# A long convolution by FFT: merged spectrum products, two copies on another engine, no idle matmuls

## The chip, the cores and the metric

The kernel runs on one core of a Trainium2 chip. Its engines run side by side, each through its own queue in order: TensorE (PE, with its weight loads shown apart as PEld) multiplies matrices into PSUM; VectorE (DVE), ScalarE (ACT) and GpSimd (POOL) work elementwise; SyncE (SP) and POOL issue the DMAs here. The metric is the device time in microseconds of one execution. Before the change it is 2101.66 us, the median of three runs (2099.22 to 2106.14).

## The reference

Two steps on `x` of 8 x 5696 x 128. First a causal convolution along the sequence, done with FFTs of twice its length; then a mixing layer with two 5696 x 5696 matrices.

```python
def _attn_ref(x, h):
    B, S, D = x.shape
    L = 2 * S
    Xf = np.fft.rfft(x, n=L, axis=1)
    Hf = np.fft.rfft(h, n=L, axis=0)
    Yf = Xf * Hf[None, :, :]
    return np.fft.irfft(Yf, n=L, axis=1)[:, :S, :].astype(np.float32)

def _moe_ref(x, w_theta, w_tok_r, w_tok_i, w_ch):
    theta = x @ w_theta
    zr, zi = x * np.cos(theta), x * np.sin(theta)
    yr = np.einsum('ts,bsd->btd', w_tok_r, zr)
    yi = np.einsum('ts,bsd->btd', w_tok_i, zi)
    u = x + yr + yi
    return (u + np.maximum(u @ w_ch, 0.0)).astype(np.float32)
```

## The kernel before

**The FFT as matmuls.** The transform of length 11392 is factored into 178 x 64. The filter `h` goes through the first two stages once; its spectrum is parked in HBM (`hf_hbm`). Then come eight groups, each two batch entries (`bp`) and half of the 128 channels (`dh`), with `dh` changing fastest. The text numbers them 0 to 7; the even ones have `dh` 0. A group has four stages:

- *Stage A* (L194): 64 matmuls of 180 columns, with slices of `x16` as weights, 4 to a PSUM tile; the 16 tiles are copied to `a_` on ScalarE (L201).
- *Stage B* (`stage_b`): 12 chunks over the 90 frequencies, 8 in each of the first 11 and 2 in the last. `f2` (L212) does a chunk's second transform in 32 matmuls (8 in the last); ScalarE copies the PSUM tile to `xs` (L310); VectorE multiplies `xs` twice by the filter's spectrum `hs`, once with its real part into `u_t` and once with its imaginary part into `v_t` (L312). `hs` comes by two DMAs a chunk on SP's queue, four chunks ahead (`LEAD`), into four buffers.
- *Stage C* (L328, L329): 256 matmuls that read all of `u_t` and `v_t` as weights, 16 to a PSUM tile; VectorE, and ScalarE for four tiles, evict them to `g` (L336, L333, L334). A matmul of stage C reads columns from every chunk, so that none can start before the last product of stage B.
- *Stage D* (`stage_d`, L351): the last inverse transform in 7 chunks over the 64 phases, 10 in each of the first 6 (20 matmuls) and 4 in the last; ScalarE copies each PSUM tile to `yt` (L354), 890 elements per partition in a full chunk, and `yt` goes to HBM.

**What runs beside what.** `woven` interleaves lists of steps by their place between 0 and 1, and a scheduler then sets the order on each engine. Stage C of a group is woven with stage A of the next, and stage B of the next group with stage D of this one. In the last group there is no next one: its stages C and D are woven with phase steps (the `theta`, sine and cosine part of the mixing layer). All these stages share one pool of four PSUM tiles, used in turn; `xs` has two buffers.

**The idle matmuls.** Behind the last chunk of stage B, and likewise behind the last chunk of the filter's pass, `f2` issues `WARM` = 12 matmuls of 384 columns (L218) whose results are not read. They write to free columns of the last chunk's PSUM tile and read `w_t2`.

**Setup.** Before the groups, tables of sines and cosines are made by POOL (L150, L152), VectorE (L155, L156, L163) and ScalarE (L160, L167): `w_t2`, `r_u`, `r_v`, `e_t`. The filter's chunks are scaled on VectorE or ScalarE in turns (L246, L248).

**The mixing layer** follows: phase steps, and from about 560 us on the products with the token matrices, in two passes of Strassen-like sums (L1099), whose weights POOL's queue loads into a ring of six buffers (L509) that takes the place of `w_t2`.

Of the kernel before, what the change touches and what calls it, by code (L numbers as in the profile page):

```python
# [12 lines left out]
F16 = mybir.dt.float16  # L13
add = mybir.AluOpType.add
mult = mybir.AluOpType.mult
AF = mybir.ActivationFunctionType
# [6 lines left out]
def kernel(  # L23
# [10 lines left out]
    nc = tc.nc  # L34
    B, S, D = x.shape
    assert D == 128
    P = 128
# [42 lines left out]
    K1 = N1 // 2 + 1  # L80
    CK = 8
    HD = D // 2
    EN = N2 // 2 + 1
    WARM = 12
    assert N1 * N2 == NF and NB * N2 == S and NB % 2 == 1 and K1 <= P
    CHK = [(c0, min(CK, K1 - c0)) for c0 in range(0, K1, CK)]
    NCK = len(CHK)
    CN = 10
    CHN = [(c0, min(CN, N2 - c0)) for c0 in range(0, N2, CN)]
    UVW = 2 * HD * K1  # L90
# [6 lines left out]
    def psum():  # L97
        return fp.tile([P, 2, 512], F32, tag="ps", name="ps")
# [3 lines left out]
    def pool(name, bufs, stack, **kw):  # L102
        return stack.enter_context(tc.tile_pool(name=name, bufs=bufs, **kw))
# [6 lines left out]
    fc = pool("fft_c", 1, conv, side="right")  # L110
# [1 line left out]
    s1 = pool("set_1", 1, setup, side="right")  # L112
    s2 = pool("set_2", 2, setup, side="right")

    u_t = fc.tile([P, UVW + P], F16)
    v_t = fc.tile([P, UVW + P], F16)
    uv = [t[:, :UVW].rearrange("p (e d k) -> p e d k", e=2, k=K1) for t in (u_t, v_t)]
    h16 = s1.tile([P, 2, N2, HD], F16)
    for p0, p1 in ((0, 80), (80, NB)):
        nc.gpsimd.dma_start(u_t[p0:p1, :N2 * D],  # L120
# [22 lines left out]
    def turns_of(pattern, base, lanes, m, per, quarter=None):  # L143

        n = 1
        for _, c in pattern:
            n *= c
        t = s2.tile([P, 11 * NB], F32, tag="turn", name="turn")[:m, :n]
        k = s2.tile([P, 11 * NB], F32, tag="whole", name="whole")[:m, :n]
        nc.gpsimd.iota(k, pattern=pattern, base=base, channel_multiplier=0,  # L150
                       allow_small_or_imprecise_dtypes=True)
        nc.gpsimd.tensor_scalar(t, k, lanes, 1.0 / per, op0=mult, op1=mult)  # L152
        if quarter is not None:
            quarter(t)
        nc.vector.tensor_scalar(k, t, MAGIC, None, op0=add)  # L155
        nc.vector.scalar_tensor_tensor(t, k, MAGIC, t, op0=ALU.subtract, op1=ALU.subtract)  # L156
        return t, k
# [12 lines left out]
    t, k = turns_of([[1, K1]], 0, lane[:NB, 1:2], NB, N1)  # L170
# [3 lines left out]
    w_t2 = keep.tile([P, K1, 3 * N2], F16, tag="keep", name="w_t2")  # L174
# [29 lines left out]
    def f2(a_st, c):  # L204

        c0, ck = CHK[c]
        ps = psum()
        for j in range(ck):
            for ri in range(2):
                for e in range(2):  # L210
                    rows = slice(64 * e, 64 * e + 64)
                    nc.tensor.matmul(ps[:, e, j * HD:(j + 1) * HD],  # L212
                                     w_t2[rows, c0 + j, N2 * (1 - ri):N2 * (3 - ri)],
                                     a_st["a"][rows, ri * K1 + c0 + j, :],
                                     start=(ri == 0), stop=(ri == 1))
        if c == NCK - 1:
            for n in range(WARM):
                nc.tensor.matmul(ps[:, n % 2, ck * HD:ck * HD + 384], w_t2[:, 2, :P],  # L218
                                 w_t2[:, 0:2, :].rearrange("p k n -> p (k n)"), start=True, stop=True)
        return ps[:, :, :ck * HD].rearrange("p e (k d) -> p e d k", k=ck)  # L220

    def woven(*lists):
# [17 lines left out]
    def h_chunk(c):  # L240
        c0, ck = CHK[c]
        ps = f2(a_h, c)
        h_ = hst[c // 6][:, c % 6]
        dst = h_[:, :, :, :ck]
        if c % 2:
            nc.vector.tensor_scalar(dst, ps, 16.0 / NF, None, op0=mult)  # L246
        else:
            nc.scalar.activation(dst, ps, AF.Copy, scale=16.0 / NF)  # L248
        for cc, j in ((0, 0), (NCK - 1, CHK[-1][1] - 1)):
            if c == cc:  # L250
                nc.vector.tensor_scalar(dst[:, :, :, j], dst[:, :, :, j], 0.5, None, op0=mult)
        for ri in range(2):
            nc.sync.dma_start(
                hf_hbm[:, c, :, ri, :].rearrange("h p n -> p h n"),
                h_[64 * ri:64 * ri + 64].rearrange("p h d k -> p h (d k)"))

    for c in range(NCK):
        h_chunk(c)
    nc.gpsimd.memset(u_t[:, UVW:], 0.0)
    nc.gpsimd.memset(v_t[:, UVW:], 0.0)  # L260

    r_u = fc.tile([P, P], F16)
    r_v = fc.tile([P, P], F16)
# [30 lines left out]
    def stage_b(a_st, dh):  # L294

        hs_of = {}

        def load(c):
            if c >= NCK:
                return  # L300
            hs = hs_of[c] = fh.tile([P, 2, HD * CK], F16, tag="hs", name="hs")
            for e in range(2):
                nc.sync.dma_start(hs[64 * e:64 * e + 64], hf_hbm[dh, c])

        def chunk(c):
            c0, ck = CHK[c]
            hv = hs_of[c].rearrange("p r (d k) -> p r d k", k=CK)
            ps = f2(a_st, c)
            xs = fs.tile([P, 2, HD, CK], F16, tag="xs", name="xs")
            nc.scalar.activation(xs[:, :, :, :ck], ps, AF.Copy)  # L310
            for r in range(2):
                nc.vector.tensor_tensor(  # L312
                    uv[r][:, :, :, c0:c0 + ck], xs[:, :, :, :ck],
                    hv[:, r:r + 1, :, :ck].to_broadcast([P, 2, HD, ck]), op=mult)
            load(c + LEAD)
        return [lambda c=c: load(c) for c in range(LEAD)], [lambda c=c: chunk(c) for c in range(NCK)]
# [22 lines left out]
    def stage_d(st, bp, dh, then=None):  # L339
        def chunk(n0, cn):  # L340
            if n0 == 0:
                st["yt"] = fg.tile([P, NB, N2], BF16, tag="yt", name="yt")
            g_, yt = st["g"], st["yt"]
            ps = psum()
            nq = 5 if cn == CN else cn
            for j in range(cn):
                n = n0 + j
                o = ps[:, j // nq, (j % nq) * NB:(j % nq + 1) * NB]
                for ri in range(2):
                    e_ = e_t[:K1, n, ri, :] if n < EN else e_t[:K1, N2 - n, ri, ::-1]  # L350
                    nc.tensor.matmul(o, g_[:K1, ri * N2 + n, :], e_, start=(ri == 0), stop=(ri == 1))  # L351
            y_out = yt[:, :, n0:n0 + cn].rearrange("p m (a q) -> p m a q", q=nq)
            y_in = ps[:, :cn // nq, :nq * NB].rearrange("p a (q m) -> p m a q", q=nq)
            nc.scalar.activation(y_out, y_in, AF.Copy)  # L354
            if n0 + cn == N2:
                if then is not None:
                    then(yt)
                if then is not None:
                    gate = nc.gpsimd.tensor_copy(small(0, 1)[HD:HD + 1], sides["phases"][1][HD:HD + 1, 3, H - 1:H]).ins
                for e in range(2):  # L360
                    t0 = H if then else 0
                    with tc.issue_after(gate) if then else ExitStack():
                        (nc.gpsimd if then else nc.sync).dma_start(
                            yt_hbm[dh * HD:(dh + 1) * HD, 2 * bp + e, t0:],
                            yt[64 * e:64 * e + 64].rearrange("p m n -> p (m n)")[:, t0:])
        return [lambda n0=n0, cn=cn: chunk(n0, cn) for n0, cn in CHN]
# [125 lines left out]
    def small(at, n):  # L492
        return ring["all"][:, WB + BT + at:WB + BT + at + n]
# [436 lines left out]
    for i, (k, p, tt, j0, s0, nj) in enumerate(stretches):  # L930
# [38 lines left out]
        if tt is None:  # L969
            if p:  # L970
                aside(True, False)
            if first_of_pair:
                q = M1 if p else M3
                ps = mps.tile([P, 512], F32, tag=f"m{q}", name=f"m{q}")
# [3 lines left out]
            for j in range(nj):  # L978
                jj = j0 + s0 + j
                for r in range(2):  # L980
# [3 lines left out]
                    for k_ in range(2):  # L984
                        for h, t in enumerate(terms):
                            nc.tensor.matmul(ps[64 * h:64 * h + 64], t[2 * k_][:, j, :64, r], b[t[2 * k_ + 1]],  # L986
                                             start=st_ and k_ == 0, stop=sp_ and k_ == 1)
# [6 lines left out]
            if end_of_pair:  # L994
# [5 lines left out]
                c, c0 = c_last  # L1000
# [48 lines left out]
        if classic:  # L1049
            for n in range(4):  # L1050
# [4 lines left out]
                if end_of_pair and n % 2:  # L1055
                    (c12, z12), (c21, z21), (c11, z11), (c22, z22) = cs
                    out_of = (((c11, z11, 0), (c12, z12, 1)), ((c21, z21, 2), (c22, z22, 3)))[n // 2]
                    for h, (c, z, m_) in enumerate(out_of):
# [6 lines left out]
                        else:  # L1065
                            for b in range(4):
                                nc.tensor.matmul(ms[m_][:, b * D:(b + 1) * D], z[:, b, :], ident_bf,
                                                 start=False, stop=(b == 3))
# [11 lines left out]
        else:  # L1080
# [13 lines left out]
            for n, q in enumerate(ORDER):  # L1094
                sum_some(1)
                for j in range(nj):
                    jj = j0 + s0 + j
                    for r in range(2):
                        nc.tensor.matmul(ms[q], a[q][:, j, :, r], bts[jj][q][:, r, :],  # L1099
                                         start=(jj == 0 and r == 0),  # L1100
                                         stop=(jj == NJ - 1 and r == 1 and q not in left))
# [60 lines left out]
```

## Time and profile before

| | |
|---|---|
| median of three runs | 2101.66 us |
| span of the profiled execution | 2098.1 us |
| PE busy | 1979.5 us, 94% |
| DVE busy | 1595.2 us, 76% |
| ACT busy | 675.3 us, 32% |
| POOL busy | 912.5 us, 43% |
| first stage C to last (L328, first starts) | 88.4 to 388.8 us |
| idle matmuls (L218) | 108, from 50.7 to 384.6 us |
| xs copies (L310) on ACT | 96, 96.6 us busy |
| spectrum products (L312) on DVE | 192; those of 1024 elements 736 and 756 ns in the mean |
| yt copies (L354) on ACT | 48 of 890 elements, 927 ns; 8 of 356, 530 ns |
| stage C evictions (L336) on DVE | 92, of 1.21 to 1.30 us in the mean |

A line of the page's groups reads: source line, engine, operation, what it writes and reads with partitions x elements and type, count; then busy time, mean duration in ns; then the engine's idle time just before these instructions and what ended it. The view of one line lists the shortest, median and longest duration and who waited for it. In the timeline each row has its start and length in us. In the rows by stretches the busy time of PE, PEld, DVE, ACT and POOL (with counts) is followed by the TensorE clock that was granted as a share of full speed, the DMA engines' busy share and GB/s.

### The profile page before, as it was taken

Reading aid. Unit: us, or ns where it says so; the run is one execution under the profiler, and the core shown is the slowest. Engines: PE = TensorE matmul, PEld = TensorE weight load, DVE = VectorE, ACT = ScalarE, POOL = GpSimd, SP = SyncE. Lnnn points to the kernel's source line nnn. Section 1 sums busy time; section 2 is a strip of 40 time slices with the busy share of each in tenths; the row PEclk is TensorE's granted clock in tenths of the full one; section 3 lists DMA queues with packets and bytes.
Section 4 is the critical chain, followed back from the end, with each engine's and each line's share of the span. In section 5 each row is a group of like instructions: output and inputs, shape, how many; then the busy total and the mean of one; then the engine's idle time right before and its main releaser. Section 6 shows DMA issues by size and latency. Waiting matters only on the chain.

```text
span 2098.1 us, 41505 instructions
## 1 busy us (share of the span) xinstructions
PE 1979.5 (94%) x15688; PEld 1109.4 (53%) x15865; DVE 1595.2 (76%) x2881; ACT 675.3 (32%) x995; POOL 912.5 (43%) x1662
## 2 busy tenths in 40 slices
PE   4888999878999999999999999899999999999998
PEld 3788888754444444444444444344444444444444
DVE  7777776776878888888886766886777777777867
ACT  5887877874332333333310000011111111111111
POOL 5301010327444636354557554435354545445450
PEclk8799999989999999999999999999999999999999
DMA  7357474989989989898999989869797887879693
GB/s 144 94 137 175 123 171 121 239 243 239 179 153 179 178 175 168 171 173 177 171 175 152 154 167 284 136 107 156 127 154 132 148 142 136 154 130 155 126 155 89
DMA packets 408233, 334.97 MB, mean 160 GB/s; under 512 B 85895, under 2 KB 358407, under 8 KB 407047
## 3 DMA queue, kind: packets, MB, share of 16 engines
q0 software_dynamic: 225952, 156.72, 52.8%
q1 hardware_dynamic: 176096, 164.05, 27.3%
q10 hardware_dynamic: 5984, 11.54, 1.6%
q8 instruction: 124, 2.03, 0.4%
q14 instruction: 77, 0.63, 0.1%
HBM read 377.11 MB, written 92.49 MB: 224 GB/s over the span
## 4 chain that ended last, share of the span: by engine, by line
PE 63%; DVE 4%; DMA 2%; issue 2%; POOL 0%; ACT 0%; DVEq 0%
PE m L1099 59%; DVE c L1106 2%; DMA ring<-in_moe_w_tok_r_dram 1%; DVE b L655 1%; PE v L801 1%; PE utp L794 1%; PE m L1103 1%; DVE wt L714 1%; PE tpz L742 0%; PE theta_ps L396 0%; POOL ring L509 0%; PE m L986 0%; DMA yT<-yt_hbm 0%; PE m L1020 0%; DMA zl<-zl_hbm 0%
## 5 line engine op out<-in xcount | busy, mean ns | idle before, releaser
L509 POOL DMA_DIRECT2D ring<-in_moe_w_tok_i_dram x720 | 390.8, 557 | 653.0 <-DVE wt L714 579.6
L509 POOL DMA_DIRECT2D ring<-in_moe_w_tok_r_dram x720 | 389.0, 559 | 145.8 <-DVE wt L714 85.5
L714 DVE STREAM_TRANSPOSE wt<-ring 128x384 f32<-128x384 f32 (+2 forms) x720 | 359.3, 523 | 110.3 <-PE m L1099 70.0
L1099 PE MATMUL m<-b,wt 128*128 128x512 bf16 x1599 | 385.9, 380 | 4.1 <-DVE wt L714 1.7
L1099 PEld LDWEIGHTS <-wt 128*128 128x128 bf16 x1804 | 176.4, 98 | 219.7 <-DVE wt L714 7.8
L1106 DVE TENSOR_TENSOR c<-c,m 128x512 f32<-128x512 f32 x412 | 265.2, 669 | 0.4 <-PE m L1099 0.4
L796 ACT ACTIVATE ring<-utp 128x512 bf16<-128x512 bf16 x85 | 50.8, 597 | 582.3 <-PE utp L794 582.3
L328 PE MATMUL ps<-r_u,u_t 128*128 128x128 f16 x1024 | 126.4, 223 | 6.4 <-ACT red L419 3.0
L329 PE MATMUL ps<-r_v,v_t 128*128 128x128 f16 x1024 | 125.5, 223 | 0.4
L1020 PE MATMUL m<-b,wt 128*128 128x512 bf16 x466 | 110.2, 381 | 8.9 <-DMA b<-z_hbm 4.9
L791 ACT ACTIVATE ub<-c 128x512 bf16<-128x512 f32 x88 | 55.0, 628 | 191.5 <-DMA ring<-in_moe_w_tok_r_dram 113.0
L130 POOL DMA_DIRECT2D x<-in_x_dram x64 | 33.9, 536 | 184.9 <-PE ps L194 174.8
L328 PEld LDWEIGHTS <-u_t 128*128 128x128 f16 x1024 | 103.4, 101 | 5.5 <-DVE u_t L312 4.6
L329 PEld LDWEIGHTS <-v_t 128*128 128x128 f16 x1024 | 102.4, 100 | 4.4 <-issue 2.4
L310 ACT ACTIVATE xs<-ps 128x1024 f16<-128x1024 f32 x96 | 96.6, 1030 | 14.7 <-DVE v_t L312 6.7
L312 DVE TENSOR_TENSOR u_t<-xs,hs 128x1024 f16<-128x1024 f16 x96 | 68.6, 715 | 29.2 <-ACT xs L310 19.0
L1020 PEld LDWEIGHTS <-wt 128*128 128x128 bf16 x528 | 51.1, 99 | 69.2 <-issue 9.6
L194 PE MATMUL ps<-f_t,x 89*128 89x180 f16 x512 | 77.2, 298 | 4.0 <-ACT xs L310 2.6
L212 PEld LDWEIGHTS <-w_t 64*128 64x128 f16 x3240 | 60.8, 102 | 37.5 <-issue 24.5
L398 ACT ACTIVATE red<-theta_ps,magic 128x512 f32<-128x512 f32 (+1 forms) x46 | 31.6, 687 | 134.6 <-PE theta_ps L396 104.5
L194 PEld LDWEIGHTS <-x 89*128 89x128 f16 x512 | 70.8, 241 | 5.5 <-issue 4.5
L744 ACT ACTIVATE ring<-tpz 128x512 bf16<-128x512 bf16 (+1 forms) x46 | 27.5, 597 | 131.9 <-PE tpz L742 113.0
(2895 smaller groups left out, 3868.9 us busy)
## 6 DMA issues: line engine op xcount, KB each, us to landing
ring<-in_moe_w_tok_r_dram POOLq DMA_DIRECT2D x352, 96.0 KB, 4.5
ring<-in_moe_w_tok_i_dram POOLq DMA_DIRECT2D x352, 96.0 KB, 4.9
ring<-in_moe_w_tok_r_dram POOLq DMA_DIRECT2D x352, 80.0 KB, 4.5
ring<-in_moe_w_tok_i_dram POOLq DMA_DIRECT2D x352, 80.0 KB, 3.9
hs<-hf_hbm SPq DMA_DIRECT2D x192, 128.0 KB, 3.1
cp_hbm<-c SPq DMA_DIRECT2D x88, 256.0 KB, 2.5
c<-cp_hbm SPq DMA_DIRECT2D x88, 256.0 KB, 4.4
out_dram<-c SPq DMA_DIRECT2D x88, 256.0 KB, 4.5
```

Source lines behind the costliest of these rows:

```text
L194: nc.tensor.matmul(ps[:, i // 2, (i % 2) * 2 * K1:(i % 2 + 1) * 2 * K1], lhs(q + i), f1_t[:NB], start=True, stop=True)
L212: nc.tensor.matmul(ps[:, e, j * HD:(j + 1) * HD], w_t2[rows, c0 + j, N2 * (1 - ri):N2 * (3 - ri)], a_st["a"][rows, ri * K1 + c0 + j, :], s ...
L310: nc.scalar.activation(xs[:, :, :, :ck], ps, AF.Copy)
L312: nc.vector.tensor_tensor(uv[r][:, :, :, c0:c0 + ck], xs[:, :, :, :ck], hv[:, r:r + 1, :, :ck].to_broadcast([P, 2, HD, ck]), op=mult)
L328: nc.tensor.matmul(o, u_t[:, at:at + P], r_u, start=True, stop=False)
L329: nc.tensor.matmul(o, v_t[:, at:at + P], r_v, start=False, stop=True)
L509: nc.gpsimd.dma_start(wb[32 * i:32 * i + 32, :ng, :nj * 64], bass.AP(tensor=a.tensor, offset=a.offset + row0 * S + p * H + i * QR + j0 * 6 ...
L714: nc.vector.transpose(wt.rearrange("p j t r -> p (j t r)").bitcast(F32).rearrange("p (j g t) -> p g j t", j=TJ, g=4)[:, :ng, :nj], wb[:, : ...
L791: nc.scalar.activation(ub[:m].rearrange("p b d -> p (b d)"), c[:m], AF.Copy)
L1020: nc.tensor.matmul(ms[n // 2 * 2 + h], a[n][:, j, :, r], bts_of[p][jj][n % 2 * 2 + h][:, r, :], start=(n % 2 == 0 and jj == 0 and r == 0), ...
L1099: nc.tensor.matmul(ms[q], a[q][:, j, :, r], bts[jj][q][:, r, :], start=(jj == 0 and r == 0), stop=(jj == NJ - 1 and r == 1 and q not in left))
L1106: nc.vector.tensor_tensor(c, z, ms[q], op=op)
```

## The change

It has three parts, all in the FFT. The idle matmuls are gone. `u_t` and `v_t` become two views of one tile `uv_t`, so that the first 11 chunks of each stage B form both products in one VectorE instruction of 2048 elements, which reads `xs` and `hs` with broadcast strides; the last, short chunk keeps two. Of stage D's seven copies those of the first and the fourth chunk go to VectorE.

```diff
-    WARM = 12
...
-    u_t = fc.tile([P, UVW + P], F16)
-    v_t = fc.tile([P, UVW + P], F16)
-    uv = [t[:, :UVW].rearrange("p (e d k) -> p e d k", e=2, k=K1) for t in (u_t, v_t)]
+    uv_t = fc.tile([P, 2 * UVW + P], F16)
+    u_t, v_t = uv_t[:, :UVW + P], uv_t[:, UVW:]
+    uv = uv_t[:, :2 * UVW].rearrange("p (r e d k) -> p (r e) d k", r=2, e=2, k=K1)
...
-        if c == NCK - 1:
-            for n in range(WARM):
-                nc.tensor.matmul(ps[:, n % 2, ck * HD:ck * HD + 384], w_t2[:, 2, :P],
-                                 w_t2[:, 0:2, :].rearrange("p k n -> p (k n)"), start=True, stop=True)
...
-    nc.gpsimd.memset(u_t[:, UVW:], 0.0)
-    nc.gpsimd.memset(v_t[:, UVW:], 0.0)
+    nc.gpsimd.memset(uv_t[:, 2 * UVW:], 0.0)
...
-            for r in range(2):
+            if ck == CK:
                 nc.vector.tensor_tensor(
-                    uv[r][:, :, :, c0:c0 + ck], xs[:, :, :, :ck],
+                    uv[:, :, :, c0:c0 + ck],
+                    xs.rearrange("p e d k -> p e (d k)").unsqueeze(1).to_broadcast([P, 2, 2, HD * CK]),
+                    hv.rearrange("p r d k -> p r (d k)").unsqueeze(2).to_broadcast([P, 2, 2, HD * CK]), op=mult)
+            for r in range(2 if ck < CK else 0):
+                nc.vector.tensor_tensor(
+                    uv[:, 2 * r:2 * r + 2, :, c0:c0 + ck], xs[:, :, :, :ck],
                     hv[:, r:r + 1, :, :ck].to_broadcast([P, 2, HD, ck]), op=mult)
...
-            nc.scalar.activation(y_out, y_in, AF.Copy)
+            if n0 in (0, 3 * CN):
+                nc.vector.tensor_copy(y_out, y_in)
+            else:
+                nc.scalar.activation(y_out, y_in, AF.Copy)
```

The last 38 columns that stage C's last matmul on `u_t` reads behind its end were zeros and are now `v_t`'s first columns; the rows that they make are not read.

## The prediction

> **What bounds the kernel now.** I read the profile in this order: the costliest groups, to see which of the edited lines are large; the lines' own views (who waits for them); the timeline across one group boundary; and sums over hand-cut stretches. The chain of waits comes last and says that, from 597 us on, the weight-mixing matmuls of L1099 set the end (59% of the span); the change does not touch them. The edited code ends at about 440 us, so all that it can do is to start the rest earlier or later, one for one. In that part the eight groups follow each other every 42 to 44 us (stage C's first matmul at 88.4, 131.1, 173.2, 216.3, 258.4, 303.0, 345.6 and 388.8 us). Each is a stage C of 21.4 to 22.9 us, followed by a stage of B and D woven, about 20.6 us from its first matmul to the next group's stage C.
>
> ```profile
> L310 ACT ACTIVATE xs<-ps 128x1024 f16<-128x1024 f32 x96 | 96.6, 1030 | 14.7 <-DVE v_t L312 6.7
> L312 DVE TENSOR_TENSOR u_t<-xs,hs 128x1024 f16<-128x1024 f16 x96 | 68.6, 715 | 29.2 <-ACT xs L310 19.0
> ```
>
> These page lines are the chain in stage B: ScalarE copies a chunk out of PSUM (xs), VectorE multiplies it twice. VectorE waits 19.0 us in all for that copy, ScalarE 6.7 us for VectorE: both are nearly full, neither is the bound alone. The view of the idle matmuls of L218:
>
> ```profile
> L218 PE MATMUL ps<-w_t x108: 326/326/527, 50.7 to 384.6; 128*128 128x384 f16 x108
> ...
>   ACT xs L310: 2.7, 3
>   DVE v_t L246: 1.6, 1
> ```
>
> They write into the last chunk's PSUM tile, so the copy of that chunk must wait for them: 2.7 us in three groups. The timeline at the end of the fourth group shows how (start, length, engine, line; in brackets the idle time before it):
>
> ```profile
> 211.97 2.12 PE L218 MATMUL ps<-w_t 128*128 128x384 f16 x12
> 212.01 1.02 ACT L310 ACTIVATE xs<-ps 128x1024 f16<-128x1024 f32 x1 [0.20 <-PE ps L212]
> ...
> 213.68 1.17 DVE L312 TENSOR_TENSOR v_t<-xs,hs 128x1024 f16<-128x1024 f16 x1
> ...
> 214.18 1.30 ACT L310 ACTIVATE xs<-ps 128x256 f16<-128x256 f32 x1 [1.15 <-PE ps L218]
> 214.22 1.78 PEld L194 LDWEIGHTS <-x 89*128 89x128 f16 x12
> ...
> 215.52 0.73 DVE L312 TENSOR_TENSOR u_t<-xs,hs 128x256 f16<-128x256 f16 x1 [0.67 <-ACT xs L310]
> ...
> 216.31 0.23 PE L328 MATMUL ps<-r_u,u_t 128*128 128x128 f16 x1 [0.15 <-DVE u_t L312]
> ```
>
> The last copy could have started at 213.03 and started at 214.18; stage C starts as soon as the last product is there. Stage A's weight loads (L194, from 214.22) slow whatever runs beside them: this copy of 256 elements takes 1.30 us here and 0.40 in other groups, a product 1.17 us for 0.69. Last, the stretches (length, then busy time by engine, granted clock, DMA share and rate): stage C of the second and third group, and the two windows around the latter's start:
>
> ```profile
> 131.06:152.44 21.38, 21.31 (x313) 21.08 (x314) 14.43 (x12) 17.65 (x23) 0.00 (x0) 1.00 0.38 101
> 173.15:195.21 22.06, 21.98 (x308) 21.64 (x310) 14.10 (x12) 14.19 (x22) 7.77 (x15) 0.92 0.80 170
> ...
> 170.98:174.41 3.43, 2.31 (x25) 2.02 (x25) 2.42 (x4) 3.11 (x6) 0.00 (x0) 1.00 0.47 126
> 174.41:177.82 3.41, 3.41 (x29) 3.41 (x29) 1.33 (x1) 2.17 (x3) 0.00 (x0) 0.50 1.04 243
> ```
>
> Stage C keeps TensorE busy throughout, so its clock counts: after a stretch with 1.1 us of idle time the clock is 0.50 for 3.41 us.
>
> **The change part by part.** In the instruction order of the two programs TensorE's is the same but for the 108 idle matmuls and a few places where stage A and C interleave; nothing is moved past a queue of SP or POOL, and no DMA is added. Joining u_t and v_t in one tile costs nothing: stage C needs every product anyway. One memset of 0.2 us less on an idle POOL: 0.
>
> (a) *No idle matmuls, odd groups.* In groups 1, 3 and 5 (12 stage A matmuls ahead of C) last F matmul to stage C takes 4.3 to 4.5 us, and 2.12 (idle) + 0.49 (last D) + 1.90 (stage A) = 4.5: TensorE itself sets it, and the last copy is held too. Without them the products set it, and the gain is the wait above: between 0 (the products are late anyway) and 2.1 x 3 = 6.4; I take -2.7. In the even groups that distance is 5.9 to 7.6 us, TensorE idles and the products set it: 0, hidden by VectorE.
>
> (b) *No idle matmuls in the setup.* After the filter's pass they run at half clock, 12 x 326 ns = 3.9 us, and hold stage A of the first group. But its first product (69.15 us) waits for the e_t tables, whose POOL work runs from 53.1 to 64.2 us and is not touched; that cover leaves 0 to -3.9, I take -1.5.
>
> (c) *One product instead of two.* A pair takes 1.30 us from the start of the first to the end of the second (196.93 to 198.22). Two-input 16-bit rows: 768 elements 557 ns (L723), 1024 elements 681 ns (L655); so 2048 at the same slope, 681 + 1024 x 124/256 = 1177 ns, say 1.19 from L312's own 693. Saved: 0.11 x 11 = 1.2 us a group. Upper bound of its cost: one element a time as in rows that read fp32, L431's 512 elements 689 and L336's 1024 about 1215, so 2048 about 2.27 us, +0.97 each. All operands stay 16-bit with unit innermost step, as in the row of before, so I take the low end.
> The second product starts 0.61 us after the first, which lasts 0.69. The Trainium skill's "VectorE: DVE Perf Modes", section "The DRAIN you can't avoid", says that the next operation waits until the pipe is empty; two would then cost 1.38 and merging would save 0.19 each, 17 us in all; the rows show the overlap, and 0.11.
>
> (d) *Two copies to VectorE.* On ScalarE 890 elements take 927 ns. On VectorE the nearest row is L199 (720 elements, fp32 PSUM to 16 bit, strided): 895 ns, so 895 x 890/720 = 1.11 as upper bound, and by the slope to L336 (1024 elements, about 1215) 895 + 170 x 320/304 = 1.07, which I take. VectorE gets 2.14 a group and loses 1.2; ScalarE loses 1.85. Placement decides: the first copy comes right behind the first product, where VectorE idles in each group (198.22 to 199.57, 1.35 us), so it costs nothing, and ScalarE's second xs no longer queues behind it, which brings the second product about 0.3 us earlier; without that hole it would cost 1.07. The second copy, ahead of the seventh product, is added in full. Together per group: -1.2 + 1.07 - 0.3 = -0.4. Bounds: -1.85 (ScalarE alone the bound) and +0.9 (VectorE alone, no hole). What is late next is the seventh product, then its hs buffer's reload (SP, 4 to 5 us from a product's end to the landing four chunks on; waits of 8.4 us in all today). Seven groups: -3, from -13 to +6.
>
> (e) *The last D stage* (421 to 440 us) has no stage B, but phase steps: ScalarE is busy 16.91 of 19 us, VectorE 11.84. Two copies less: up to -1.9, I take -1.5 (0 if TensorE, 17.07 of 19, holds it).
>
> (f) *The clock.* The idle matmuls fill a third of each boundary. Today stage C starts or soon falls to 0.50 in groups 0, 2, 4 and 6, never in 1, 3, 5. Price of one window: 22.06 - (21.38 - 4 x 0.15) = 1.3 us (the even groups have 4 stage A matmuls less left, 0.15 us each); of two, as in group 6 (22.90): 2.1. Between 0 and 7 x 2.1 - (3 x 1.3 + 2.1) = +8.7; I take one more window, +1.3.
> On this the Trainium skill's "TensorE: Matmul & The Clock Gate", Part 1, speaks of about 3.4 us without work before the clock is halved. No boundary idles so long, so by that page the term is 0; but the row at 170.98 was 2.31 of 3.43 us busy and was followed by 0.50.
>
> Sum: -2.7 - 1.5 - 3 - 1.5 + 1.3 = -7.4 us on the profiled execution's 2098.1. The runs' median, 2101.66, lies 3.6 above that span (launch and spread); carried over, 2094.
>
> **The rivals.** *It cancels* (2099). For it: the loops are tightly coupled (two xs buffers, four hs buffers, four PSUM tiles), so relief of ScalarE is only used as far as VectorE follows, and a product chain that is already full takes (d) at -0.1; and each odd group that wins 0.9 in (a) loses 1.3 in (f). By letter: -2.7 - 1.5 - 0.7 - 1.5 + 3.9 = -2.5. Against it: VectorE idles some 4 us of each 20 today.
>
> *Stage C starts at half clock everywhere* (slower, about 2113). Without the idle matmuls TensorE has 0.49 + 1.9 to 2.5 us of work in the 4.5 to 6 us before stage C, and an idle stretch ahead of C is followed by a low window that reaches into C; if the window that C starts in isn't full either, one more follows: 2.1 + 3.41/2 = 3.8 us a group. 7 x 3.8 - 6 = +20.6; with the -8.7 of the other terms +12. It outweighs the gains from (8.7 + 6)/7 = 2.1 us a group on, and by 0.3% from 3.0 on. For it: the third group's row. Against: a window amid B and D that was no busier, 2.29 of 3.41 us from 205.1 on, kept the clock at 1.00.
>
> *VectorE becomes the bound* (slower, about 2108): +0.9 a group and 0.5 of later hs reloads, 8 x 1.4 = 11, less 4.2 from (a) and (b). For it: a pair of products takes 1.3 us and each group has twelve. Against: the hole after the first product.
>
> *The merged product falls to one element a time* (about 2180): 88 x 0.97 = +85, on VectorE alone. Then the edit would not do what it says; the row of before speaks against it.
>
> **How the numbers follow.** Forecast (faster, 2094): 0.45, its own range 2082 to 2095.3. It cancels, within 0.3% (6.3 us, about what a measurement of this kernel can tell from no change): 0.27. Clock 0.13, VectorE 0.10, one element 0.05: slower 0.28. The sum of the best ends is -21 (2081), of the worst without the last rival about +15 (2117). The range 2081 to 2115 leaves out the last rival and the ends of the others.
>
> **What would show it.** One product row of 1.18 us (2.27: the last rival); VectorE copies of 1.07; no wait of ScalarE for L218; the distance from last F matmul to stage C down to 3.3 in groups 1, 3 and 5; first F matmul to stage C 20.2 rather than 20.6; granted clock in groups 1, 3, 5 at 1.00 but for one window. I am wrong if stage B takes as long as before (VectorE full, hs waits up), or if stages C grow beyond 22.1.

## The result, and the profile after

| | before | changed |
|---|---|---|
| median of the runs (us) | 2101.71 | 2106.66 |
| lowest to highest | 2099.02 to 2106.14 | 2103.32 to 2111.83 |
| ratio to before, 95% interval | | 1.0028, 1.0015 to 1.0042 |
| span of the profiled execution | 2098.1 | 2102.3 |

The changed kernel is slower by 0.28%, some 6 us (5.0 between the medians), where the forecast was 7.6 us faster. Two groups of the page after, its instruction views (count: least, median and longest ns, first and last start, shape), with the waits ahead of them:

```profile
L306 DVE TENSOR_TENSOR uv_t<-xs,hs 128x2048 f16<-128x2048 f16 x88 | 114.2, 1331 | 19.3 <-ACT xs L304 12.3
...
L304 ACT ACTIVATE xs<-ps 128x1024 f16<-128x1024 f32 x96 | 94.9, 1021 | 26.4 <-PE ps L211 16.5
```

```profile
L306 DVE TENSOR_TENSOR uv_t<-xs,hs x88: 1215/1226/2251, 70.2 to 390.1; 128x2048 f16<-128x2048 f16 x88
```

```profile
L354 DVE CAST yt<-ps x16: 1077/1078/1085, 114.0 to 433.1; 128x890 bf16<-128x890 f32 x16
```

(L304 is the xs copy, L306 the merged product, L354 the copy on VectorE, L211 stage F, which is `f2`'s matmuls in stage B; they were L310, L312, L354 and L212 before.) The prices are the forecast ones: 1.226 us for the product, 1.078 us for the copy. VectorE waits 12.3 us for xs where it was 19.0. But ScalarE, relieved, now waits 16.5 us for stage F's matmuls. The same wait in the view of before's L310 (us in all, times):

```profile
  PE ps L212: 2.9, 5
```

The loss stands in the stretches of stage C, groups 1 and 3 (length; then busy time of PE, PEld, DVE, ACT, POOL; clock, DMA share, rate):

```profile
131.04:153.66 22.62, 22.62 (x312) 22.34 (x314) 14.48 (x12) 16.83 (x23) 0.00 (x0) 0.92 0.36 93
216.98:240.53 23.55, 23.55 (x313) 23.27 (x315) 14.43 (x12) 16.71 (x22) 0.00 (x0) 0.87 0.34 87
...
127.65:131.07 3.42, 1.71 (x13) 1.42 (x13) 3.24 (x4) 3.42 (x6) 0.00 (x0) 1.00 0.62 166
131.07:134.48 3.41, 3.41 (x30) 3.23 (x31) 1.53 (x2) 1.68 (x3) 0.00 (x0) 0.50 1.06 246
212.99:216.40 3.41, 2.04 (x17) 1.86 (x13) 3.10 (x2) 3.41 (x6) 0.00 (x0) 1.00 0.68 190
216.40:219.81 3.41, 2.83 (x24) 2.65 (x25) 1.53 (x4) 1.63 (x3) 0.00 (x0) 0.50 0.98 236
219.81:223.23 3.42, 3.42 (x31) 3.42 (x30) 2.05 (x2) 1.89 (x3) 0.00 (x0) 0.50 0.93 241
```

Both stages took 21.38 us before, at full clock. Now the window of 3.41 us that ends within 0.6 us of each one's start is 1.71 and 2.04 us busy, and the clock is 0.50 for one window in group 1 (22.62 us) and for two in group 3 (23.55). The boundary itself, in the timeline (start, length, engine, line; in brackets the idle time before):

```profile
127.45 0.65 PE L193 MATMUL ps<-f_t,x 89*128 89x180 f16 x4
128.71 1.98 DVE L306 TENSOR_TENSOR uv_t<-xs,hs 128x2048 f16<-128x2048 f16 x1 [0.18 <-ACT xs L304]
128.73 0.62 PE L193 MATMUL ps<-f_t,x 89*128 89x180 f16 x4 [0.64 <-ACT xs L304]
...
130.57 0.95 DVE L311 TENSOR_TENSOR uv_t<-xs,hs 128x256 f16<-128x256 f16 x2
131.04 0.29 PE L327 MATMUL ps<-r_u,uv_t 128*128 128x128 f16 x1 [0.90 <-DVE uv_t L311]
```

Stage A's few matmuls are spread over the time in which the idle ones stood; the last products still set stage C's start, since the last big one takes 1.98 us beside stage A's weight loads. All kernels' stages, each from one profile, in us (C: stages C of groups 0 to 6 together; F to C: the end of one stage C, where stage F's matmuls begin, to the next stage C, groups 1 to 7 together; D end: the end of the last stage D):

```
kernel                                     C    F to C   D end
before                                 153.25   147.15   434.6
changed                                159.18   145.33   437.4
e1_no_idle_only                        157.83   149.73   440.6
e2_idle_kept                           153.21   145.92   433.5
e3_merge_only                          152.71   147.80   431.9
e4_copies_only                         153.15   149.04   438.0
e5_first_copy                          155.91   144.61   434.1
e6_idle_behind_d                       152.05   146.70   431.8
e7_idle_more                           149.55   153.08   433.4
e8_few_columns                         158.90   149.40   439.7
e9_change_idle_d                       150.18   148.77   430.2
e10_first_copy_d                       151.01   145.37   428.6
e11_idle_d_only                        150.62   147.86   428.8
e12_quarter_rows                       158.59   149.48   440.5
```

From before to the changed kernel, stages C of groups 0 to 6 grow by 5.9 us and the way to them shrinks by 1.8. Each is one profile: a single long wait in one group moves the second column by 2 us and more, while the first follows the clock and is steadier.

### The profile page after: what moved, and what is told of

The parts are those of the page before. It is cut to its first block, busy times and chain, and to the rows that moved or that the text cites. A ratio compares the mean times of both kernels' runs of the same rounds, so it can differ in the third digit from the quotient of the medians.

```text
span 2102.3 us, 41195 instructions
## 1 busy us (share of the span) xinstructions
PE 1969.5 (94%) x15580; PEld 1105.2 (53%) x15757; DVE 1605.9 (76%) x2809; ACT 661.2 (31%) x979; POOL 907.6 (43%) x1661
## 4 chain that ended last, share of the span: by engine, by line
PE 63%; DVE 4%; DMA 3%; issue 2%; POOL 1%; ACT 0%; DVEq 0%; POOLq 0%
PE m L1101 58%; DMA ring<-in_moe_w_tok_r_dram 2%; DVE c L1108 1%; DVE b L657 1%; PE v L803 1%; PE utp L796 1%; PE m L1105 1%; POOL ring L511 1%; DVE wt L716 1%; PE theta_ps L398 0%; PE tpz L744 0%; PE m L988 0%; PE m L1022 0%; DMA zl<-zl_hbm 0%; DMA wl<-in_moe_w_tok_i_dram 0%
## 5 line engine op out<-in xcount | busy, mean ns | idle before, releaser
L327 PE MATMUL ps<-r_u,uv_t 128*128 128x128 f16 x1024 | 132.1, 229 | 7.0 <-DVE uv_t L311 5.4
L328 PE MATMUL ps<-r_v,uv_t 128*128 128x128 f16 x1024 | 131.0, 228 | 0.1
L306 DVE TENSOR_TENSOR uv_t<-xs,hs 128x2048 f16<-128x2048 f16 x88 | 114.2, 1331 | 19.3 <-ACT xs L304 12.3
L327 PEld LDWEIGHTS <-uv_t 128*128 128x128 f16 x1024 | 106.3, 104 | 8.8 <-DVE uv_t L311 8.8
L328 PEld LDWEIGHTS <-uv_t 128*128 128x128 f16 x1024 | 105.4, 103 | 2.6 <-DVE uv_t L311 1.5
L304 ACT ACTIVATE xs<-ps 128x1024 f16<-128x1024 f32 x96 | 94.9, 1021 | 26.4 <-PE ps L211 16.5
L193 PE MATMUL ps<-f_t,x 89*128 89x180 f16 x512 | 81.6, 313 | 10.4 <-ACT xs L304 7.6
L211 PEld LDWEIGHTS <-w_t 64*128 64x128 f16 x3240 | 60.8, 102 | 38.6 <-issue 26.0
L193 PEld LDWEIGHTS <-x 89*128 89x128 f16 x512 | 73.4, 233 | 12.3 <-issue 11.4
```

The costliest lines, as they stand in the source:

```text
L193: nc.tensor.matmul(ps[:, i // 2, (i % 2) * 2 * K1:(i % 2 + 1) * 2 * K1], lhs(q + i), f1_t[:NB], start=True, stop=True)
L211: nc.tensor.matmul(ps[:, e, j * HD:(j + 1) * HD], w_t2[rows, c0 + j, N2 * (1 - ri):N2 * (3 - ri)], a_st["a"][rows, ri * K1 + c0 + j, :], s ...
L306: nc.vector.tensor_tensor(uv[:, :, :, c0:c0 + ck], xs.rearrange("p e d k -> p e (d k)").unsqueeze(1).to_broadcast([P, 2, 2, HD * CK]), hv. ...
L327: nc.tensor.matmul(o, u_t[:, at:at + P], r_u, start=True, stop=False)
L328: nc.tensor.matmul(o, v_t[:, at:at + P], r_v, start=False, stop=True)
```

## The experiments

Theory 1: the idle matmuls held the TensorE clock over the group boundaries, and their loss costs more than their time. The rival: the merged products or the copies on VectorE make the loss. The first four kernels take the change apart.

**e1_no_idle_only**: before, without the idle matmuls.

```diff
-        if c == NCK - 1:
-            for n in range(WARM):
-                nc.tensor.matmul(ps[:, n % 2, ck * HD:ck * HD + 384], w_t2[:, 2, :P],
-                                 w_t2[:, 0:2, :].rearrange("p k n -> p (k n)"), start=True, stop=True)
```

> Only the idle matmuls are taken out; products and copies as before. Theory 1 (the idle matmuls held the TensorE clock across the group boundaries): stages C of groups 1, 3 and 5 start at half clock and take 22.6 to 23.5 us instead of 21.4, some 4 to 6 us in all; against that stand 2 to 4 us of shorter boundaries and setup; time 0 to +4 us against before (2102 to 2106). Rival (the merged products or the VectorE copies make the loss, by hs waits and a full VectorE): the clock costs one window at most, and this kernel gains 3 to 4 us (2098).

Measured: ratio 1.0019 (1.0011 to 1.0028), 4.0 us slower. Stages C of groups 1, 3 and 5 took 23.12, 22.85 and 22.58 us. Theory 1's numbers; the rival's gain is excluded.

**e2_idle_kept**: the whole change, with the four lines above put back.

> The whole change, but with the idle matmuls kept as before. Theory 1: stages C last as before (21.4 and 22.1 us), first F matmul to next stage C is 0.4 to 0.7 us shorter in most groups, time 3 to 7 us below before (2095 to 2099). Rival: 3 to 8 us above before (2105 to 2110), with longer hs waits of VectorE than the 8.4 us of before.

Measured: 0.9998 (0.9987 to 1.0009). The loss is gone, but so is theory 1's gain: neither expectation met. Products and copies together bring nothing that can be measured. So the sum was wrong in a second place.

**e3_merge_only**: e2 without the copies on VectorE.

```diff
-            if n0 in (0, 3 * CN):
-                nc.vector.tensor_copy(y_out, y_in)
-            else:
-                nc.scalar.activation(y_out, y_in, AF.Copy)
+            nc.scalar.activation(y_out, y_in, AF.Copy)
```

> Only the merged product; copies on ScalarE and idle matmuls as before. A product takes 1.22 us for a pair's 1.30: theory 1 gives 0 to -3 us (2099 to 2102). Rival: a product lands later for its first half and the hs reload with it, +2 to +5 us (2104 to 2107).

Measured: 0.9983 (0.9972 to 0.9995), 3.6 us faster, from 1.1 to 5.9 by the interval: the merge gains, a little beyond the 0 to -3 expected.

**e4_copies_only**: before, with the copies' four lines alone.

> Only the two copies on VectorE (1.08 us each); two products per chunk and idle matmuls as before. Theory 1: -1 to -4 us (2098 to 2101), of it 1 to 2 us in the last stage D. Rival: VectorE is full, +2 to +5 us (2104 to 2107).

Measured: 1.0003 (0.9995 to 1.0012): no change, between both. Where the copies' gain goes can be looked for in e2 beside e3, which differ in them alone (0.9998 and 0.9983; the intervals overlap, so a cost of theirs isn't clear of noise). The view of the xs copy over groups 1 to 7, for e3 and then for e2:

```profile
L309 ACT ACTIVATE xs<-ps x84: 404/1052/1615, 110.2 to 384.6; 128x1024 f16<-128x1024 f32 x77, 128x256 f16<-128x256 f32 x7
...
  PE ps L212: 3.5, 8
```

```profile
L309 ACT ACTIVATE xs<-ps x84: 398/1023/1612, 109.9 to 383.5; 128x1024 f16<-128x1024 f32 x77, 128x256 f16<-128x256 f32 x7
...
  PE ps L212: 15.3, 17
```

ScalarE's wait for stage F goes from 3.5 to 15.3 us: what it no longer copies, it waits. VectorE's wait for xs goes from 22.6 to 11.4 us in the same stretch, 11.2 less, and 14 copies of 1.08 us, 15.1 in all, are added to it. The timeline of one group (stage B behind group 3's stage C) shows both copies, e2 first:

```profile
241.53 1.00 PE L355 MATMUL ps<-e_t,g__4371 90*128 90x89 f16 x20 [0.83 <-DVE g__4371 L340]
...
241.80 1.23 DVE L311 TENSOR_TENSOR uv_t<-xs,hs 128x2048 f16<-128x2048 f16 x1 [0.41 <-ACT xs L309]
...
242.47 1.11 PE L212 MATMUL ps<-a__4352,w_t 64*128 64x64 f16 x64
...
242.94 1.08 DVE L359 CAST yt<-ps 128x890 bf16<-128x890 f32 x1
...
243.20 1.94 ACT L309 ACTIVATE xs<-ps 128x1024 f16<-128x1024 f32 x2 [1.43 <-PE ps L212]
...
250.67 1.08 DVE L359 CAST yt<-ps 128x890 bf16<-128x890 f32 x1
...
252.03 2.49 DVE L311 TENSOR_TENSOR uv_t<-xs,hs 128x2048 f16<-128x2048 f16 x2 [0.28 <-DMA hs<-hf_hbm]
```

```profile
241.68 1.23 DVE L311 TENSOR_TENSOR uv_t<-xs,hs 128x2048 f16<-128x2048 f16 x1 [0.41 <-ACT xs L309]
...
242.50 0.92 ACT L358 ACTIVATE yt<-ps 128x890 bf16<-128x890 f32 x1 [0.86 <-PE ps L355]
...
243.31 1.93 ACT L309 ACTIVATE xs<-ps 128x1024 f16<-128x1024 f32 x2
...
251.21 2.36 DVE L311 TENSOR_TENSOR uv_t<-xs,hs 128x2048 f16<-128x2048 f16 x2 [0.34 <-DMA hs<-hf_hbm]
```

Both are read from the group's first product, at 241.80 in e2 and 241.68 in e3. The second xs copy starts 1.40 us after it and not 1.63: 0.23 us is all that the free ScalarE is worth, since stage F's second chunk is behind stage D's first on TensorE (241.53), and that waits for stage C's last result on VectorE. The seventh product starts 10.23 us after the first, not 9.53, and the way to stage C takes 20.86 us in e2 and 20.08 in e3. But both seventh products waited last for the load of `hs`, which in e2 landed at 251.91, 0.16 us after the copy's end: this group doesn't price the copy. Group 6 does. Its rows in e2 and then in e10, which is told below and has the first copy alone on VectorE:

```profile
326.91 1.23 DVE L311 TENSOR_TENSOR uv_t<-xs,hs 128x2048 f16<-128x2048 f16 x1 [0.41 <-ACT xs L309]
...
335.78 1.08 DVE L359 CAST yt<-ps 128x890 bf16<-128x890 f32 x1
...
336.78 1.22 DVE L311 TENSOR_TENSOR uv_t<-xs,hs 128x2048 f16<-128x2048 f16 x1
```

```profile
322.30 1.23 DVE L307 TENSOR_TENSOR uv_t<-xs,hs 128x2048 f16<-128x2048 f16 x1 [0.41 <-ACT xs L305]
...
330.03 2.49 DVE L307 TENSOR_TENSOR uv_t<-xs,hs 128x2048 f16<-128x2048 f16 x2 [0.28 <-ACT xs L305]
```

In e2 the seventh product follows the second copy without idle time, 9.87 us after the first product; in e10 it is the second of the last row's two, at 331.30, 9.00 us after; in e3, with no copy there, 9.22. So the first copy brings it 0.22 us earlier and the second 0.87 later. Even so, this group's way to stage C is no longer in e2 (20.36 us) than in e3 (20.47): what the delay costs at the end isn't shown.

**e5_first_copy** was to price the two copies apart.

```diff
-            nc.scalar.activation(y_out, y_in, AF.Copy)
+            if n0 == 0 or (n0 == 3 * CN and then is not None):
+                nc.vector.tensor_copy(y_out, y_in)
+            else:
+                nc.scalar.activation(y_out, y_in, AF.Copy)
```

> The merged product with the idle matmuls kept, and of the copies only the first of a group on VectorE, in the hole behind the first product; the second one only in the last stage D, where no stage B runs. Theory 2 (it is the second copy of a group, ahead of the seventh product, that costs what the copies cost; the last stage D gains from both): time 0 to 3 us below the kernel with the merged product alone (0.998 to 0.997 of before). Rival (a copy on VectorE costs wherever it stands, since ScalarE, relieved, only waits for stage F's matmuls): 2 to 4 us above that kernel (1.000).

Measured: 0.9989 (0.9976 to 1.0002), beside e3's 0.9983: inconclusive; the last stage D gained nothing (below).

**e6_idle_behind_d**: e3 with the idle matmuls moved.

```diff
+            if n0 + cn == N2 and then is None:
+                for n in range(WARM):
+                    nc.tensor.matmul(ps[:, 1, :384], w_t2[:, 2, :P],
+                                     w_t2[:, 0:2, :].rearrange("p k n -> p (k n)"), start=True, stop=True)
```

(with e1's lines out; the new ones stand in stage D, ahead of its copy)

> The merged product alone, with the 12 idle matmuls moved from the PSUM tile of stage B's last chunk to that of stage D's last chunk (none in the setup and in group 0): the same columns run at the same place in TensorE's order, or one stage D chunk later, but the last copy of stage B no longer waits for them. Theory 1: stages C keep their length (21.4 in odd groups), the distance last F matmul to stage C falls by some 0.7 in odd groups, time 1 to 4 us below the kernel with the merged product alone. Rival (the wait has no price, since the last products are late anyway): same time as that kernel, to 1 us.

Measured: 0.9986 (0.9976 to 0.9996), as e3. Stages C keep 21.4 us, but the distance in odd groups doesn't fall (4.99, 5.30, 4.00 us for e3's 4.36, 5.00, 4.44): the rival's answer.

**e7_idle_more**: e6 with `range(WARM if dh == 0 and bp < B // 2 - 1 else 20)`.

> As the kernel with idle matmuls behind stage D, but 20 of them in place of 12 ahead of stages C of groups 2, 4, 6 and 7. Theory 1: a window of 3.41 us needs some 4,700 columns streamed, so 8 x 384 = 3,072 more keep most of these at full clock: stages C of groups 2, 4 and 6 go from 22.0 to about 21.1 us, 2 to 4 us less than with 12. Rival: the matmuls themselves come late (1.4 us each time) and eat the gain: same to +3 us.

Measured: 0.9989 (0.9980 to 0.9997). As expected, stages C of groups 2, 4 and 6 run at full clock, 21.13, 21.00 and 20.86 us. The time doesn't follow: in its profile the way from F to C is 6.4 us longer than in e6, by longer ways in groups 1, 4, 6 and 7 (21.93, 22.01, 22.31, 24.50 us). Whether more idle matmuls cause these isn't settled; ahead of group 1 their number is as in e6.

**e8_few_columns**: before, with `range(2 * WARM)` idle matmuls of 64 columns.

> The kernel before, with 24 idle matmuls of 64 columns in place of 12 of 384: TensorE is busy as long (24 weight loads of 0.09 us for 2.1 us), with 1,536 columns for 4,608. Theory 1 (the clock follows the columns streamed in a window): stages C of groups 1, 3 and 5 start at half clock, 22.6 us and more, time as without idle matmuls or above, +3 to +8 us. Rival (the clock follows idle time, so any matmul will do): stages C of 21.4 us, time as before within 2 us.

Measured: 1.0016 (1.0005 to 1.0027); stages C of groups 1, 3 and 5 took 22.64, 23.69 and 22.79 us. Its premise was wrong, though: the 24 matmuls take 0.87 us, not 2.1, as their weight loads overlap; so it doesn't tell columns from busy time.

To find what the clock follows, all the windows were counted. The clock's edges in each profile lie on a grid of 3.413 us, within 0.01 us. For each window between 100 and 376 us that began at full clock, in all 14 profiles, the sum over its matmuls of columns x rows / 128 (idle 384; C 128; A 180 x 89/128 = 125; D 63; F 32; a matmul partly inside by its share) was set against the clock of the next window:

```
rows x columns/128     windows   next at half clock
under 3080                  76        76
3080 to 3120                 5         1
3120 to 4000                86         0
over 4000                  852         0

PE busy (us of 3.41)   windows   next at half clock
under 2.0                   44        41
2.0 to 2.5                  67        26
2.5 to 3.0                 235         7
over 3.0                   673         3
```

The first measure tells the next clock in 1018 of 1019 windows; busy time doesn't. The bound of 3,080 was on record before e9 to e12 ran, and their 297 windows, 19 of them below it, have no exception. e7's bound, 4,700 columns without the rows, doesn't hold: of 78 windows below it 20 stayed at full clock, and of 941 above it 19 were followed by half. The largest sum in a full window was 7,827, so the bound is near 39% of that. The weights of all these matmuls span 128 columns of the array, so whether that side counts isn't told. e12 tests the rows by themselves.

**e12_quarter_rows**: before, its idle matmuls on 32 rows.

```diff
-                nc.tensor.matmul(ps[:, n % 2, ck * HD:ck * HD + 384], w_t2[:, 2, :P],
-                                 w_t2[:, 0:2, :].rearrange("p k n -> p (k n)"), start=True, stop=True)
+                nc.tensor.matmul(ps[:, n % 2, ck * HD:ck * HD + 384], w_t2[:32, 2, :P],
+                                 w_t2[:32, 0:2, :].rearrange("p k n -> p (k n)"), start=True, stop=True)
```

> The kernel before, with idle matmuls of 32 rows in place of 128: the same number, the same 384 columns, a quarter of the array's rows. If the clock follows columns alone, as before (stages C of groups 1, 3 and 5 at 21.4 us, within 2 us). If it follows rows times columns (a window of 3.41 us needs about 3,080 columns of 128 rows), the boundary windows of before, recounted so, come to 1,890 to 2,660 in six of seven groups, and these fall to half clock: stages C of 22.5 us and more or a longer way to them, +3 to +8 us (1.0015 to 1.004).

Measured: 1.0023 (1.0012 to 1.0034). Its timeline ahead of group 1's stage C, and two windows:

```profile
128.78 2.12 PE L218 MATMUL ps<-w_t 32*128 32x384 f16 x12
```

```profile
128.65:132.06 3.41, 3.41 (x41) 2.34 (x34) 3.27 (x5) 3.19 (x5) 0.00 (x0) 1.00 0.46 123
132.06:135.48 3.42, 2.90 (x22) 2.28 (x22) 1.91 (x4) 2.62 (x5) 0.00 (x0) 0.50 0.54 156
```

The block takes 2.12 us, as with 128 rows, and TensorE is busy for all of the window; yet the next is at 0.50. The window streams 6,882 columns, but only 2,646 by rows x columns. Columns alone, busy time and idle time are out; rows x columns stands. The time is that of e1 (1.0019), although the idle matmuls are all there and as long as before: it is the clock that costs, not their place in TensorE's order.

**e9_change_idle_d**: the changed kernel plus e6's lines (12 idle matmuls).

> The whole change, with 12 idle matmuls put back behind stage D's last chunk (groups 1 to 7). Theory 1 and 2: the clock is kept as in the kernel that has the merged product with the idle matmuls there, so stages C of groups 1, 3 and 5 take 21.4 us, and what is left against that kernel is the price of the two copies, 1 to 3 us: 0.999 to 1.000 of before. Rival (the copies gain once the clock is kept): 0.996 to 0.998.

Measured: 0.9983 (0.9974 to 0.9992), between the two expectations and as e6: here the copies show neither a cost nor a gain. Stages C of groups 1 and 3:

```profile
129.52:150.90 21.38, 21.30 (x313) 21.07 (x315) 14.95 (x12) 16.67 (x23) 0.00 (x0) 1.00 0.39 99
213.96:235.33 21.37, 21.30 (x313) 21.06 (x315) 14.43 (x12) 16.67 (x23) 0.00 (x0) 1.00 0.37 99
```

Only the idle matmuls differ from the changed kernel, whose ratio was 1.0028: 0.45%, some 9.5 us (6 to 13 with both intervals taken together), of which stages C of groups 0 to 6 show 9.0 (159.18 to 150.18).

**e10_first_copy_d**: e6 with the first copy of groups 0 to 6 on VectorE.

```diff
-            nc.scalar.activation(y_out, y_in, AF.Copy)
+            if n0 == 0 and then is None:
+                nc.vector.tensor_copy(y_out, y_in)
+            else:
+                nc.scalar.activation(y_out, y_in, AF.Copy)
```

> The merged product with the idle matmuls behind stage D, and the first copy of each group but the last on VectorE. Theory 2 (ScalarE, relieved, waits for stage F's matmuls instead): same as without that copy, 0.9985 to 0.999 of before. Rival (the hole behind the first product is worth 0.3 us a group): 2 us less, 0.9975 to 0.998.

Measured: 0.9979 (0.9967 to 0.9992), the fastest of all, 4.4 us below before; e6 and e9 lie within its interval, so this doesn't tell the first copy's worth. It beats before and the changed kernel alike.

**e11_idle_d_only**: before, with e1's lines out and e6's in.

> The kernel before, with its 12 idle matmuls moved behind stage D's last chunk (none in the setup and in group 0), products and copies as before. If ScalarE's wait for them (2.7 us) and their 3.9 us in the setup were on the path, 2 to 4 us below before (0.998 to 0.999); if the last products are late anyway, as before (1.000).

Measured: 0.9990 (0.9979 to 1.0002), 2.1 us below, and not apart from no change.

## Why the prediction was wrong

The failing step is (f), the clock, taken at +1.3 us with "one more window". With the idle matmuls out, stage C starts at half clock or falls to it at once in each of groups 0 to 6. Stages C of these groups grow by 5.9 us against before, and the removal costs 4.0 us alone (e1) and some 9.5 against a kernel that has the same edits and idle matmuls behind stage D (e9). The bounds, 0 to +8.7, held the 5.9; the value taken was near their low end, and (f) gives no reason for one window. The one argument against more stands with the rival: "a window amid B and D that was no busier, 2.29 of 3.41 us from 205.1 on, kept the clock at 1.00". Recounted, that window of before holds 3,300, its neighbour in the argument, at 170.98, 3,050 with 2.31 us busy: one on each side of the bound. Busy time was the wrong unit. The price of a window was right: 1.24 us for group 1's one (22.62 - 21.38), 2.17 for group 3's two.

So the rival *stage C starts at half clock everywhere* came true in its mechanism, not in its size. Its 3.8 us a group, less the 6 lost before, made +20.6; the 5.9 and these 6 make 1.7 a group. That is under the 2.1 from which it was to outweigh the gains, but the gains were not there either.

The other terms:

- (a) and (b), -4.2 together. e11 moves the idle matmuls where they hold no copy up and is 2.1 us faster (from 4.4 faster to 0.4 slower); its stages C show 2.6 of that (150.62 for 153.25), so its one profile leaves nothing for the wait that was to go. In the odd groups the distance to stage C was to fall to 3.3 us; in the changed kernel it is 4.07, 5.14 and 4.62. The zero bound of (a), late products, held: 16 products of the changed kernel ran beside stage A's weight loads and took 1.31 to 2.25 us, the two last big ones of each odd group among them, where the median is 1.226. For (b), stage C of group 0 starts at 87.4 us on average in the seven kernels with no idle matmuls up to there (the changed one, e1, e6, e7, e9 to e11) and at 88.2 in before and e2 to e5: 0.8, with single values 3 us apart.
- (c), 1.2 us a group, 8.4 in seven. Direction right, size not: the product measured 1.226 for 1.19, so a chunk saves 0.07 and not 0.11, and e3 gained 3.6 us, 0.5 a group. The rival of one element a time (2.27 us) is out.
- (d), 1.07 - 0.3 = 0.77 a group. The copies last 1.078 us, and in group 6 the hole gave 0.22 and the second copy cost 0.87, together 0.65, up to the seventh product. With (c) at its measured size, (c) and (d) are not -3 but about nothing, which is e2's 0.9998. That the delay of the seventh product reaches stage C isn't shown: over all groups the runs leave the copies between nothing (e9 beside e6) and 3 us (e2 beside e3), neither clear of noise. *VectorE becomes the bound* isn't shown either; a loss of its size is excluded by e2.
- (e), -1.5, is gone. From stage C's end to the last D matmul it is 14.9 to 16.5 us in the kernels with both copies there (the changed one, e2, e4, e5, e9) and 13.3 to 15.4 in the other nine. ScalarE's load of 16.91 of 19 us was an average; the wait that ends last there is another one. Two waits of TensorE in this stretch, before and changed:

```profile
PE ps L351 <- ACT red L419: 2.5, 1, 2.5
```

```profile
PE ps L350 <- DVE g__8346 L335: 2.1, 1, 2.1
```

The first is for a phase step on ScalarE, the second for stage C's result on VectorE, which the copy there doesn't shorten.

With what was measured, (a) and (b) are about 0 to -0.8, (c) -3.6, (d) and (e) 0 to +3.2, and (f) +5.9: +1.5 to +5.5, and the runs say +5.9, from 3.2 to 8.8. That stages C grow beyond 22.1 us was named in the forecast as a sign of error, and that came. One sum in the range was off as well: the best ends, -6.4, -3.9, -13, -1.9 and 0, make -25 and not -21; nothing here turns on it.

## What to carry to other kernels

Idle matmuls that look like waste can be holding the clock: before taking them out, sum rows x columns over each clock window at the places they fill, and price the windows that drop. If they are in the way, move them to where nobody waits for their PSUM tile (e9: the whole change so, some 9.5 us faster than without them) rather than drop them. An engine's relief is worth only what the next wait in that place allows: read it from the timeline, counted from an event that both kernels share, not from a sum of busy times, and in more than one group: in group 4 another wait, for a load, ended just behind the copy and hid its price.

## What the runs showed of the hardware

- In these profiles the TensorE clock of the next 3.413 us window was 0.50 whenever the last one, at full clock, streamed fewer than about 3,080 columns x rows/128 (1018 of 1019 windows), whatever its busy time: 3.41 of 3.41 us busy with matmuls of 32 rows was followed by 0.50. The Trainium skill's "TensorE: Matmul & The Clock Gate", Part 1, says that the gate follows how busy the engine has been and names an idle window of about 3.4 us; the window's length agrees with these runs, the idleness doesn't.
- A matmul of 384 columns on 32 rows takes as long as one on 128: 12 of them took 2.12 us both ways.
- 24 idle matmuls of 64 columns, each with its weight load of 98 ns, took 0.87 us: weight loads overlap one another, so their sum is no bound.
